# Block 0's gate and up of the second token pair by Strassen's seven products

## The chip, the cores and the metric

The kernel runs on one core of one Trainium2 chip. The metric is device time in microseconds (us), the median of several runs of one launch. Engines are called as in the profile: PE is TensorE's matmul stream and PEld its weight loads, DVE is VectorE, ACT is ScalarE, POOL is GpSimd, SP is SyncE, which here only issues DMAs.

## The reference

Two branches over the same x (2048 tokens, width 640) are mixed by a gate; the feed-forward width is 1728.

```python
a = jnp.einsum("bsd,ed->bse", x, dft_hid_re)
b = jnp.einsum("bsd,ed->bse", x, dft_hid_im)
y = jnp.einsum("ts,bse->bte", dft_seq_re, a) - jnp.einsum("ts,bse->bte", dft_seq_im, b)   # branch A
ffn = (gelu(x @ w_gate) * (x @ w_up)) @ w_down                                             # branch B
g = sigmoid((x * gate_w).sum(-1, keepdims=True))
out = g * y + (1 - g) * ffn
```

## The kernel before, in words

Every product is done in three matmuls: a float32 operand is split into a high part (a copy to the matmul's type, on ACT, `high`) and a low part (the rest, on DVE, `low`), and `mm3` adds high x high, high x low and low x high in a PSUM bank. There are eight banks of 128 x 512. Depth 640 is five tiles of 128; the 2048 tokens are two pairs of two tiles of 512 columns (pair 0 and pair 1, tile 1 and 2 of each); the width 1728 is 13 blocks of 128 and 64 rows more. Gate and up of these last 64 stand together in one "mixed" block of 128 rows: 64 of gate, 64 of up.

The order is: block 0 and the mixed block of the feed-forward; blocks 1 to 12; the down projection; branch A. Blocks 1 to 12 do gate and up by Strassen's algorithm in Winograd's form: tiles 0 to 3 of the depth are two halves (x pieces `(1,t)` and `(2,t)`), the four quarters of the problem are gate/up by token tile, and seven products of two depth tiles stand in for eight. The fifth depth tile (`x5`) is added plainly. For it the sums T1 to T4 of x pieces (`tsum`) and S1 to S4 and D of weights (`make_w`) are made on DVE, and each is split in its turn (`his`, `lows`).

Block 0 and the mixed block (`first_products`, `first_out`) are plain in the kernel before: for each token tile, five depth tiles by three blocks (m, g, u). Pair 0 is done as its data arrive; then tile 1 and tile 2 of pair 1. In this second stage the sums T1 to T4 of pair 0, T1 and T2 of pair 1 and all of block 1's weight parts are made beside the matmuls. `first_out` takes gelu of gate rows on ACT, multiplies by up rows on DVE, and stores the hidden rows to DRAM by a POOL DMA (`keep`). The mixed rows are multiplied twice, once into each half of a 128-row tile, so that the down projection finds them in both halves.

The first stages stand in one block `in_order(ACT, DVE, PE)`, which chains the instructions of each of these engines in the order of the program; blocks 1 to 12 stand in a second one, with POOL. The two chains of an engine are not tied to each other: the framework's scheduler merges them. In the second, work that is not matmul is spread between the products from a list with costs (`fills`; `todo` is put in it first). Big tiles (`slot`) come from a pool of 46 buffers of 4 KB per partition, given out in the order of the program as they come free.

The generator `gate_up` is the Strassen order for blocks 1 to 12, one per pair, whose steps the loop interleaves: X = A11 product of both pairs, a copy of X to V by ACT, V += A12 product and the fifth depth tile, Z = S1·T1, X += S2·T2, Z += D, X += S3·T3, then `s5 += X` on DVE, Z += S4, X += A22·T4, and the multiplies.

Of the kernel before, what the change touches and what calls it, by code (L numbers as in the profile page):

```python
# [9 lines left out]
F32 = mybir.dt.float32  # L10
F32R = mybir.dt.float32r
AF = mybir.ActivationFunctionType
ALU = mybir.AluOpType

P = 128
S, D, F = 2048, 640, 1728
T = 512
NT = S // T
ND = D // P
# [4 lines left out]
FR = F - NF * P  # L24
# [13 lines left out]
def kernel(  # L38
# [27 lines left out]
    nc = tc.nc  # L66
# [5 lines left out]
    def slot(dt, shape, name):  # L72
        return pool.tile(shape, dt, tag="s4", name=name, bufs=46)

    def mtile(dt, name):
        return pool.tile([P, T], dt, tag="m", name=name, bufs=14)

    def bank(name):
        return psum.tile([P, T], F32, tag="ps", name=name, bufs=8)

    def high(hi, raw):
        nc.scalar.activation(hi, raw, AF.Copy)  # L82

    def low(hi, lo, raw):
        nc.vector.tensor_tensor(lo, raw, hi.bitcast(F32), op=ALU.subtract)  # L85
# [13 lines left out]
    def mm3(ps, lhs, rhs, first, last):  # L99
        (lh, ll), (rh, rl) = lhs, rhs  # L100
        nc.tensor.matmul(ps, lh, rh, start=first, stop=False, skip_group_check=True)  # L101
        nc.tensor.matmul(ps, lh, rl, start=False, stop=False, skip_group_check=True)  # L102
        nc.tensor.matmul(ps, ll, rh, start=False, stop=last, skip_group_check=True)  # L103
# [19 lines left out]
    gwb = pool.tile([P, D], F32, tag="gwb", name="gwb")  # L123
# [18 lines left out]
    def at(hilo, i):  # L142
        h, l = hilo
        return h[:, i], l[:, i]

    def copy(src, name):
        m = mtile(F32, name)
        nc.scalar.activation(m, src, AF.Copy)  # L148
        return m
# [3 lines left out]
    def xpart(B, d, t):  # L153
        return at(B[1 + d // 2, t], d % 2) if d < 4 else at(B[5], t - 1)
# [47 lines left out]
    def wsmall(dt, name):  # L202
        return pool.tile([P, 2, P], dt, tag="w", name=name, bufs=6)
# [8 lines left out]
    def load_w(f):  # L212


        if f >= NF:
            return
        ra, rb = slot(F32, [P, 8, P], f"wa{f}r"), wsmall(F32, f"wb{f}")
        nc.sync.dma_start(ra, wf[f - 1, :, :8])
        nc.sync.dma_start(rb, wf[f - 1, :, 8:])
        rq = None  # L220
        if pair_of(f) == 1:
            rq = slot(F32, [P, 8, P], f"wq{f}r")
            nc.sync.dma_start(rq[:, 0:2], wf[f, :, 0:2])
            nc.sync.dma_start(rq[:, 2], wf[f, :, 4])
        wraw[f] = ra, rb, rq
# [147 lines left out]
        return W, work  # L373


    FIRST = [[(0, 1), (1, 3)], [(3, 6)], [(6, 8), (8, 9)], [(9, 12)], [(12, 15)]]

    def load_first():

        r, h, l = ([slot(dt, [P, 8, P], f"w0{n}{k}") for k in range(2)] for n, dt in (("r", F32), ("h", F32R), ("l", F32R)))  # L380
        W = {n: [tuple(v[c // 8][:, c % 8] for v in (h, l)) for c in range(k, 3 * ND, 3)] for k, n in enumerate("mgu")}

        def at8(v, a, b):
            return v[a // 8][:, a % 8 : a % 8 + b - a]

        def load(engine, a, b):
            engine.dma_start(at8(r, a, b), w0[:, a:b])

        def parts(do, a, b):
            if do is high:  # L390
                high(at8(h, a, b), at8(r, a, b))
            else:
                low(at8(h, a, b), at8(l, a, b), at8(r, a, b))

        return W, load, parts

    def keep(to, i, src):
        nc.gpsimd.dma_start(to[:, i], src)  # L398

    def first_banks(tp, t):  # L400
        return {n: bank(f"p{n}{tp}{t}") for n in "mgu"}

    def first_products(bk, W, B, t, ds=range(ND)):

        for d in ds:
            for n in "mgu":
                mm3(bk[n], W[n][d], xpart(B, d, t), d == 0, d == ND - 1)

    def first_out(bk, tp, t):
        ge, hf = mtile(F32, f"gem{tp}{t}"), mtile(F32, f"hfm{tp}{t}")  # L410
        nc.scalar.activation(ge[:FR], bk["m"][:FR], AF.Gelu_apprx_tanh)
        g = mtile(F32, f"ge{tp}{t}")
        nc.scalar.activation(g, bk["g"], AF.Gelu_apprx_tanh)
        tt(hf[:FR], ge[:FR], bk["m"][FR:], op=ALU.mult)
        tt(hf[FR:], ge[:FR], bk["m"][FR:], op=ALU.mult)
        keep(h0[tp], 1 + t, hf)
        tt(g, g, bk["u"], op=ALU.mult)
        keep(h0[tp], t - 1, g)

# [559 lines left out]
            put(2 * q + 1, 0, a[q])  # L979


    W0, load_part, parts = load_first()
    Bs = []
    B, tiles, load, piece, tsum, his, lows = load_x(0)

# [23 lines left out]
    def split_piece(d, t):  # L1009
        raw, _, hilo = piece(d, t)  # L1010
        split(*hilo, raw)

    with in_order(ACT, DVE, PE):
        nc.scalar.activation(table, table, AF.Gelu_apprx_tanh)
        idle = bank("idle")
        for k in range(14):
            nc.tensor.matmul(idle[:, halves[k % 2]], *ones, start=k == 0, stop=True, skip_group_check=True)
        bk1, bk2 = first_banks(0, 1), first_banks(0, 2)
        for d in range(ND):
            raw, _, (h, l) = piece(d, 1)  # L1020
            first, *rest = FIRST[d]
            parts(high, *first)
            if d == 0:
                a, b = halves
                nc.vector.tensor_copy(h[:, a], raw[:, a])
                low(h[:, a], l[:, a], raw[:, a])
                parts(low, *first)
                split(h[:, b], l[:, b], raw[:, b])
                parts(high, *rest[0])
                parts(low, *rest[0])  # L1030
            else:
                high(h, raw)
                parts(low, *first)
                low(h, l, raw)
                for r in rest:
                    parts(high, *r)
                for r in rest:
                    parts(low, *r)
            split_piece(d, 2)
            if d == 0:  # L1040
                wh, wl = W0["m"][0]
                for c in halves:
                    order = ((wh, h), (wl, h), (wh, l)) if c is halves[1] else ((wh, h), (wh, l), (wl, h))
                    for k, (w, x) in enumerate(order):
                        first = k == 0 and c is halves[0]
                        nc.tensor.matmul(bk1["m"][:, c], w, x[:, c], start=first, stop=False, skip_group_check=True)
                for n in "gu":
                    mm3(bk1[n], W0[n][0], (h, l), True, False)
            else:
                first_products(bk1, W0, B, 1, [d])  # L1050
            if d == 0:
                h, l = xpart(B, d, 2)
                for n in "mgu":
                    for k, w in enumerate(W0[n][d]):
                        nc.tensor.matmul(bk2[n], w, h, start=k == 0, stop=False, skip_group_check=True)
                for n in "mgu":
                    nc.tensor.matmul(bk2[n], W0[n][d][0], l, start=False, stop=False, skip_group_check=True)
            else:
                first_products(bk2, W0, B, 2, [d])
        B0, (tsum0, his0, lows0) = B, (tsum, his, lows)  # L1060
        Bs.append(B)
        B, tiles, load, piece, tsum, his, lows = load_x(1)
        tiles(1)
        load(1)
        tiles(2)
        load(2)
        tsum0(1)
        his((1, 1), (2, 1))
        lows((1, 1), (2, 1))
        split_piece(4, 1)  # L1070
        first_out(bk1, 0, 1)
        first_out(bk2, 0, 2)
        bk1 = first_banks(1, 1)
        first_products(bk1, W0, B, 1)
        tsum0(3)
        his0("T1", "T3")
        lows0("T1", "T3")
        tsum0(2)
        tsum0(4)
        his((1, 2), (2, 2))  # L1080
        lows((1, 2), (2, 2))
        split_piece(4, 2)
        his0("T2", "T4")
        lows0("T2", "T4")
        first_out(bk1, 1, 1)
        load_w(1)
        W, work = make_w(1)
        for _, do in work:
            do()
        load_w(2)  # L1090
        nc.sync.dma_start(gwb, gw.to_broadcast([P, D]))
        bk2 = first_banks(1, 2)
        first_products(bk2, W0, B, 2)
        tsum(1)
        his("T1")
        tsum(2)
        his("T2")
        lows("T1")
        first_out(bk2, 1, 2)

        todo.extend([(114, partial(lows, "T2")), (114, partial(tsum, 3)), (0, partial(his, "T3"))])
        todo.extend([(114, partial(tsum, 4)), (0, partial(his, "T4"))])
        todo.extend([(114, partial(lows, "T3")), (114, partial(lows, "T4"))])
    loads.close()
    Bs.append(B)
    zq = list(range(NS))
# [74 lines left out]
    with in_order(PE, ACT, DVE, POOL):  # L1181
        for f in range(1, NF):
# [80 lines left out]
            W = nxt  # L1263
# [438 lines left out]
```

## Time and profile before

| what | value |
|---|---|
| median of 3 runs | 1020.71 us (1020.39 to 1021.24) |
| span of the profiled execution, first to last instruction | 1019.2 us |
| PE busy | 1014.9 us, 4483 matmuls |
| DVE, ACT, POOL busy | 826.7, 485.1, 163.2 us |
| mean granted TensorE clock | 1.000 |
| products of pair 0, block 0 and mixed | until 25.65 us of the span |
| products of pair 1, block 0 and mixed | 25.65 to 46.05 us |
| block 1 | 46.05 to 70.55 us |

The profile gives one execution. Its own time is its span and 1.5 us around it, if it took as long as the median run. A row of the list in order of time reads: start, duration, engine, source line, operation, output tile <- input tiles, shapes, and in brackets the idle time of the engine before it with what ended it. A line such as L82 or L101 is a helper's (`high`, `mm3`), so rows are told apart by tile names: `x111h` is the high part of x of pair 1, piece 1, tile 1; `xT12l` the low part of pair 1's T2; `wa1`, `ws1` block 1's weights and their sums; `pm`, `pg`, `pu`, `pX`, `pV`, `pZ` PSUM banks. Matmuls are pipelined: a row's duration overlaps the next row, and the distance of two starts is what one costs.

### The profile page before, as it was taken

What the parts mean: (1) busy time and instruction counts of PE and PEld (TensorE: products, weight loads), DVE (VectorE), ACT (ScalarE), POOL (GpSimd) and SP (SyncE); (2) the same over time, 40 slices, a digit from 0 to 9 for tenths busy, and PEclk for the clock granted to TensorE, in tenths of its full rate; (3) what the DMA queues carried; (4) which work ended last, traced back from release to release, by engine and by line L of the source; (5) the groups of instructions that cost most, each with busy time, mean ns of one, the idle gap of its engine ahead of it and who ended that gap; (6) DMA issues with size and microseconds to landing.
All of it is one profiled execution on the core that took longest, in us unless ns stands there. A gap on an engine that the chain in (4) does not pass through costs nothing.

```text
span 1019.2 us, 13255 instructions
## 1 busy us (share of the span) xinstructions
PE 1014.9 (100%) x4483; PEld 840.1 (82%) x4483; DVE 826.7 (81%) x1158; ACT 485.1 (48%) x618; POOL 163.2 (16%) x291
## 2 busy tenths in 40 slices
PE   9999999999999999999999999999999999999998
PEld 7888888888888888888888888888888888888887
DVE  6987887977687979988887976898488859797796
ACT  5544535353535577557444443444344345455440
POOL 0122241323221200100001012102210200021121
PEclk9999999999999999999999999999999999999999
DMA  7468577968689999968874669658866877897855
GB/s 271 168 210 274 182 270 241 311 226 280 200 286 287 407 364 413 355 233 331 295 258 173 209 242 330 218 196 296 296 209 208 300 250 273 292 350 219 273 143 89
DMA packets 96068, 265.74 MB, mean 261 GB/s; under 512 B 12608, under 2 KB 26944, under 8 KB 96000
## 3 DMA queue, kind: packets, MB, share of 16 engines
q1 hardware_dynamic: 70512, 185.24, 52.9%
q0 software_dynamic: 25200, 79.46, 23.1%
q8 instruction: 35, 0.57, 0.2%
q14 instruction: 33, 0.27, 0.1%
q10 hardware_dynamic: 288, 0.20, 0.1%
HBM read 192.48 MB, written 70.27 MB: 258 GB/s over the span
## 4 chain that ended last, share of the span: by engine, by line
PE 100%; DVE 0%; issue 0%
PE pX L102 7%; PE pX L101 7%; PE pX L103 7%; PE pZ L101 5%; PE pZ L102 5%; PE pZ L103 5%; PE pL L103 3%; PE pL L101 3%; PE pL L102 3%; PE pV L103 2%; PE pV L101 2%; PE pV L102 2%; PE pR L103 1%; PE pY L103 1%; PE pQ L103 1%; PE pQ L101 1%
## 5 line engine op out<-in xcount | busy, mean ns | idle before, releaser
L82 ACT ACTIVATE ch<-csa 128x1024 fp32r<-128x1024 f32 x32 | 34.0, 1062 | 78.5 <-DVE csa L764 77.1
L85 DVE TENSOR_TENSOR cl<-cra,ch 128x1024 fp32r<-128x1024 f32 x32 | 39.1, 1222 | 27.0 <-ACT ch L82 24.9
L82 ACT ACTIVATE ch<-cra 128x1024 fp32r<-128x1024 f32 x32 | 33.9, 1059 | 52.3 <-DVE cl L85 16.3
L85 DVE TENSOR_TENSOR cl<-crb,ch 128x1024 fp32r<-128x1024 f32 x32 | 39.1, 1223 | 14.5 <-ACT ch L82 14.5
L103 PE MATMUL pL<-ch,xal 128*128 128x512 f32 x128 | 49.8, 389 | 0.0
L102 PE MATMUL pL<-cl,xah 128*128 128x512 f32 x128 | 49.8, 389 | 0.0
L101 PE MATMUL pL<-ch,xah 128*128 128x512 f32 x128 | 49.7, 389 | 0.0
L398 POOL DMA_DIRECT2D hA<-s x48 | 26.1, 544 | 138.1 <-DVE s L556 118.5
L82 ACT ACTIVATE ch<-crb 128x1024 fp32r<-128x1024 f32 x32 | 33.8, 1055 | 29.7 <-PE pL L102 11.6
L85 DVE TENSOR_TENSOR cl<-csb,ch 128x1024 fp32r<-128x1024 f32 x32 | 39.2, 1225 | 3.7 <-ACT ch L82 2.3
L85 DVE TENSOR_TENSOR cl<-csa,ch 128x1024 fp32r<-128x1024 f32 x32 | 39.1, 1221 | 2.1 <-ACT ch L82 1.1
L82 ACT ACTIVATE ch<-csb 128x1024 fp32r<-128x1024 f32 x32 | 34.0, 1062 | 11.7 <-DVE csb L767 5.0
L550 ACT ACTIVATE s<-s 128x512 f32<-128x512 f32 x24 | 15.2, 633 | 47.6 <-DVE s L549 47.6
L148 ACT ACTIVATE s<-pX 128x512 f32<-128x512 f32 x40 | 23.7, 596 | 29.0 <-PE pX L103 28.4
L82 ACT ACTIVATE kh<-kw 128x1024 fp32r<-128x1024 f32 x24 | 25.3, 1054 | 18.9 <-DMA kw<-wsd 14.5
L85 DVE TENSOR_TENSOR kl<-kw,kh 128x1024 fp32r<-128x1024 f32 x24 | 29.3, 1220 | 4.3 <-ACT kh L82 4.3
L545 DVE TENSOR_TENSOR s<-s,pX 128x512 f32<-128x512 f32 x24 | 16.4, 685 | 19.2 <-PE pX L103 19.1
L1349 POOL DMA_DIRECT2D uA<-c x8 | 4.3, 541 | 168.9 <-DVE c L1451 168.6
L398 POOL DMA_DIRECT2D hT<-s x48 | 26.0, 541 | 18.5 <-DVE s L573 8.1
L923 POOL DMA_DIRECT2D out<-ks x12 | 6.5, 541 | 137.4 <-DVE ks L922 136.5
L102 PEld LDWEIGHTS pL<-cl,xah 128*128 128x128 f32 x128 | 24.0, 188 | 5.0
L103 PEld LDWEIGHTS pL<-ch,xal 128*128 128x128 f32 x128 | 24.0, 188 | 5.0
(3626 smaller groups left out, 3479.0 us busy)
## 6 DMA issues: line engine op xcount, KB each, us to landing
cra<-in_ct SPq DMA_DIRECT2D x64, 512.0 KB, 4.2
crb<-in_ct SPq DMA_DIRECT2D x64, 512.0 KB, 5.0
hA<-s POOLq DMA_DIRECT2D x48, 256.0 KB, 5.7
hT<-s POOLq DMA_DIRECT2D x48, 256.0 KB, 5.0
kr<-hA SPq DMA_DIRECT2D x24, 512.0 KB, 7.7
kr<-hT SPq DMA_DIRECT2D x24, 512.0 KB, 7.3
ux<-uA SPq DMA_DIRECT2D x24, 512.0 KB, 6.2
ux<-uT SPq DMA_DIRECT2D x16, 512.0 KB, 7.3
```

What stands on the lines that cost most here:

```text
L82: nc.scalar.activation(hi, raw, AF.Copy)
L85: nc.vector.tensor_tensor(lo, raw, hi.bitcast(F32), op=ALU.subtract)
L101: nc.tensor.matmul(ps, lh, rh, start=first, stop=False, skip_group_check=True)
L102: nc.tensor.matmul(ps, lh, rl, start=False, stop=False, skip_group_check=True)
L103: nc.tensor.matmul(ps, ll, rh, start=False, stop=last, skip_group_check=True)
L148: nc.scalar.activation(m, src, AF.Copy)
L398: nc.gpsimd.dma_start(to[:, i], src)
L545: tt(s5, s5, X, op=ALU.add)
L550: nc.scalar.activation(s2, s2, AF.Gelu_apprx_tanh)
L923: nc.gpsimd.dma_start(acc4[:, t] if tp and e == 4 else out[2 * tp + t, e], src)
L1349: nc.gpsimd.dma_start(to[:, i], src)
```

## The change

Pair 1 of block 0 is done by the seven products. `load_first` now loads block 0's weights into three tiles of six chunks each instead of two of eight, and its new function `strassen` makes S1 to S4 and D from them; the mixed block's plain products stand between the seven. T2 to T4 of pair 0 are moved into block 1's `todo` list, T1 to T4 of pair 1 are made in this stage, and block 1's weight parts are made at its end. The loads of blocks 1 and 2's weights and of the gate's row are issued before the stage. The mixed rows are multiplied once and stored by two DMAs of 64 rows.

```diff
-    FIRST = [[(0, 1), (1, 3)], [(3, 6)], [(6, 8), (8, 9)], [(9, 12)], [(12, 15)]]
+    FIRST = [[(0, 1), (1, 3)], [(3, 6)], [(6, 9)], [(9, 12)], [(12, 15)]]
...
+        def strassen():
+            sm, sh, sl = (slot(dt, [P, 8, P], f"ws0{n}") for n, dt in (("r", F32), ("h", F32R), ("l", F32R)))
+            d, dr = wsmall(F32R, "wd0"), wsmall(F32, "wd0r")
+            (g01, u01), (g23, u23) = ([r[k][:, q:6:3] for q in (1, 2)] for k in range(2))
+            tt(sm[:, 0:2], u01, u23, op=ALU.add)
+            tt(sm[:, 4:6], g01, u01, op=ALU.subtract)
+            tt(sm[:, 2:4], sm[:, 0:2], g01, op=ALU.subtract)
+            tt(sm[:, 6:8], g23, sm[:, 2:4], op=ALU.subtract)
+            tt(dr[:, 0], r[2][:, 1], r[2][:, 2], op=ALU.subtract)
+            high(sh, sm)
+            high(d[:, 0], dr[:, 0])
+            low(sh, sl, sm)
+            low(d[:, 0], d[:, 1], dr[:, 0])
...
+    def mixed_out(ge, m, tp, t):
+        hf = mtile(F32, f"hfm{tp}{t}")
+        tt(hf[:FR], ge[:FR], m[FR:], op=ALU.mult)
+        for q in range(2):
+            nc.gpsimd.dma_start(h0[tp][q * FR : (q + 1) * FR, 1 + t], hf[:FR])
...
         split_piece(4, 1)
+        load_w(1)
+        load_w(2)
+        nc.sync.dma_start(gwb, gw.to_broadcast([P, D]))
+        S0 = first_strassen()
         first_out(bk1, 0, 1)
         first_out(bk2, 0, 2)
-        bk1 = first_banks(1, 1)
-        first_products(bk1, W0, B, 1)
-        tsum0(3)
-        his0("T1", "T3")
-        lows0("T1", "T3")
-        tsum0(2)
-        tsum0(4)
-        his((1, 2), (2, 2))
-        lows((1, 2), (2, 2))
-        split_piece(4, 2)
-        his0("T2", "T4")
-        lows0("T2", "T4")
-        first_out(bk1, 1, 1)
-        load_w(1)
-        W, work = make_w(1)
-        for _, do in work:
-            do()
-        load_w(2)
-        nc.sync.dma_start(gwb, gw.to_broadcast([P, D]))
-        bk2 = first_banks(1, 2)
-        first_products(bk2, W0, B, 2)
-        tsum(1)
-        his("T1")
-        tsum(2)
-        his("T2")
-        lows("T1")
-        first_out(bk2, 1, 2)
-        todo.extend([(114, partial(lows, "T2")), (114, partial(tsum, 3)), (0, partial(his, "T3"))])
-        todo.extend([(114, partial(tsum, 4)), (0, partial(his, "T4"))])
-        todo.extend([(114, partial(lows, "T3")), (114, partial(lows, "T4"))])
+        x1, x2 = at(B[5], 0), at(B[5], 1)
+        X, M1 = bank("pX0_1"), bank("pm11")
+        prod(X, "A11", (1, 1), True)
+        mixed(M1, 1, range(ND))
+        V = bank("pV0_1")
+        nc.scalar.activation(V, X, AF.Copy)
+        tsum(1)
+        his("T1")
+        lows("T1")
+        split_piece(4, 2)
+        prod(V, "A12", (2, 1), False)
+        mm3(V, S0["g5"], x1, False, True)
+        tsum(2)
+        his((1, 2), "T2")
+        lows((1, 2), "T2")
+        ge = mixed_gelu(M1, 1, 1)
+        his((2, 2))
+        s1 = mtile(F32, "s10_1")
+        nc.scalar.activation(s1, V, AF.Gelu_apprx_tanh)
+        lows((2, 2))
+        mixed_out(ge, M1, 1, 1)
+        Z, M2 = bank("pZ0_1"), bank("pm12")
+        prod(Z, "S1", "T1", True)
+        mm3(Z, S0["u5"], x2, False, True)
+        s5 = copy(Z, "s50_1")
+        mixed(M2, 2, range(2))
+        prod(X, "S2", "T2", False)
+        tsum(3)
+        his("T3")
+        lows("T3")
+        s2 = copy(X, "s20_1")
+        mm3(Z, S0["D"], x2, False, False)
+        mixed(M2, 2, range(2, ND))
+        prod(X, "S3", "T3", False)
+        tsum(4)
+        his("T4")
+        lows("T4")
+        W, work = make_w(1)
+        sums, high_a, sums2, high_c, low_a, diff, low_c = (do for _, do in work)
+        high_a()
+        ge = mixed_gelu(M2, 1, 2)
+        mixed_out(ge, M2, 1, 2)
+        tt(s5, s5, X, op=ALU.add)
+        prod(Z, "S4", (2, 2), False)
+        prod(X, "A22", "T4", False)
+        mm3(X, S0["u5"], x1, False, True)
+        low_a()
+        tt(s2, s2, Z, op=ALU.add)
+        nc.scalar.activation(s2, s2, AF.Gelu_apprx_tanh)
+        sums()
+        tt(s2, s2, s5, op=ALU.mult)
+        keep(h0[1], 1, s2)
+        sums2()
+        high_c()
+        his0("T1")
+        tt(s1, s1, X, op=ALU.mult)
+        keep(h0[1], 0, s1)
+        lows0("T1")
+        low_c()
+        diff()
+        for k in (2, 3, 4):
+            todo.extend([(114, partial(tsum0, k)), (0, partial(his0, f"T{k}")), (114, partial(lows0, f"T{k}"))])
```

More of the change, by code (lines that the diff above doesn't have):

```diff
@@ L373, in make_w @@
         return W, work
-    FIRST = [[(0, 1), (1, 3)], [(3, 6)], [(6, 8), (8, 9)], [(9, 12)], [(12, 15)]]
+    FIRST = [[(0, 1), (1, 3)], [(3, 6)], [(6, 9)], [(9, 12)], [(12, 15)]]
     def load_first():
-        r, h, l = ([slot(dt, [P, 8, P], f"w0{n}{k}") for k in range(2)] for n, dt in (("r", F32), ("h", F32R), ("l", F32R)))
-        W = {n: [tuple(v[c // 8][:, c % 8] for v in (h, l)) for c in range(k, 3 * ND, 3)] for k, n in enumerate("mgu")}
+        r, h, l = ([slot(dt, [P, 8, P], f"w0{n}{k}") for k in range(3)] for n, dt in (("r", F32), ("h", F32R), ("l", F32R)))
+        W = {n: [tuple(v[c // 6][:, c % 6] for v in (h, l)) for c in range(k, 3 * ND, 3)] for k, n in enumerate("mgu")}
         def at8(v, a, b):
-            return v[a // 8][:, a % 8 : a % 8 + b - a]
+            return v[a // 6][:, a % 6 : a % 6 + b - a]
         def load(engine, a, b):
@@ L393, in parts @@
                 low(at8(h, a, b), at8(l, a, b), at8(r, a, b))
-        return W, load, parts
+        def strassen():
[11 more added lines that the diff above has]
+            low(d[:, 0], d[:, 1], dr[:, 0])
+            S = {"D": (d[:, 0], d[:, 1]), "g5": W["g"][4], "u5": W["u"][4]}
+            for i in range(2):
+                S["A11", i], S["A12", i], S["A22", i] = W["g"][i], W["g"][2 + i], W["u"][2 + i]
+                for k in range(4):
+                    S[f"S{k + 1}", i] = at((sh, sl), 2 * k + i)
+            return S
+        return W, load, parts, strassen
     def keep(to, i, src):
@@ L407, in first_products, with mixed_gelu @@
                 mm3(bk[n], W[n][d], xpart(B, d, t), d == 0, d == ND - 1)
+    def mixed_gelu(m, tp, t):
+        ge = mtile(F32, f"gem{tp}{t}")
+        nc.scalar.activation(ge[:FR], m[:FR], AF.Gelu_apprx_tanh)
+        return ge
+    def mixed_out(ge, m, tp, t):
[3 more added lines that the diff above has]
+            nc.gpsimd.dma_start(h0[tp][q * FR : (q + 1) * FR, 1 + t], hf[:FR])
     def first_out(bk, tp, t):
-        ge, hf = mtile(F32, f"gem{tp}{t}"), mtile(F32, f"hfm{tp}{t}")
-        nc.scalar.activation(ge[:FR], bk["m"][:FR], AF.Gelu_apprx_tanh)
+        ge = mixed_gelu(bk["m"], tp, t)
         g = mtile(F32, f"ge{tp}{t}")
         nc.scalar.activation(g, bk["g"], AF.Gelu_apprx_tanh)
-        tt(hf[:FR], ge[:FR], bk["m"][FR:], op=ALU.mult)
-        tt(hf[FR:], ge[:FR], bk["m"][FR:], op=ALU.mult)
-        keep(h0[tp], 1 + t, hf)
+        mixed_out(ge, bk["m"], tp, t)
         tt(g, g, bk["u"], op=ALU.mult)
@@ L979, in step_k @@
             put(2 * q + 1, 0, a[q])
-    W0, load_part, parts = load_first()
+    W0, load_part, parts, first_strassen = load_first()
     Bs = []
@@ L1084, with prod, mixed @@
-        lows0("T2", "T4")
-        first_out(bk1, 1, 1)
-        load_w(1)
-        W, work = make_w(1)
-        for _, do in work:
-            do()
-        load_w(2)
-        nc.sync.dma_start(gwb, gw.to_broadcast([P, D]))
-        bk2 = first_banks(1, 2)
-        first_products(bk2, W0, B, 2)
+        def prod(ps, a, b, first):
+            for i in range(2):
+                mm3(ps, S0[a, i], at(B[b], i), first and i == 0, True)
+        def mixed(ps, t, ds):
+            for d in ds:
+                mm3(ps, W0["m"][d], xpart(B, d, t), d == 0, True)
```

## The prediction

> **What bounds the kernel now.** I read the page first (busy shares, the chain that ended last), then busy time by window over the start, where the change lies, then the instructions there in order of time, engine by engine.
>
> ```profile
> PE 1014.9 (100%) x4483; PEld 840.1 (82%) x4483; DVE 826.7 (81%) x1158; ACT 485.1 (48%) x618; POOL 163.2 (16%) x291
> PE 100%; DVE 0%; issue 0%
> 25.65:46.05 20.40, 20.40 (x91) 16.89 (x90) 19.85 (x25) 10.19 (x13) 3.09 (x6) 1.00 0.57 209
> 46.05:70.55 24.50, 24.50 (x109) 20.26 (x108) 19.91 (x27) 12.60 (x19) 2.71 (x5) 1.00 0.48 154
> ```
>
> The last two rows give window, length, busy time and count of PE, PEld, DVE, ACT, POOL, granted clock, DMA share, GB/s. TensorE alone sets the time. The first window is the second token pair's plain stage, 90 matmuls (x91 counts a straddler) in 20.40 us: 0.2267 us each. The second is block 1, 108 matmuls. PE never waits, so a matmul saved counts in full, and so does a wait. But VectorE is busy 19.85 of 20.40 us in the stage that is rewritten.
>
> ```profile
> 25.65 0.39 PE L101 MATMUL pm<-x111h,w0h 128*128 128x512 f32 x1
> 25.88 0.39 PE L102 MATMUL pm<-x111l,w0h 128*128 128x512 f32 x1
> 46.05 0.39 PE L101 MATMUL pX<-x011h,wa1h 128*128 128x512 f32 x1
> ```
>
> **The change, part by part.** (1) Matmuls. Before: 5 depth tiles x 3 blocks x 3 x 2 token tiles = 90. After: mixed block 30, seven products 42, leftover depth tile 4 x 3 = 12: 84. Six fewer: -6 x 0.2267 = -1.36 us. The Trainium skill ("TensorE: Matmul & The Clock Gate", "Wait — 56ns, not 53.3ns?") gives 215.7 ns for such a matmul; an estimate from that page would be -1.29; the rows decide.
>
> (2) VectorE and ScalarE up to the new products:
>
> ```profile
> 19.38 0.69 DVE L85 TENSOR_TENSOR x15l<-xr,x15h 128x512 fp32r<-128x512 f32 x1
> 23.08 0.69 DVE L414 TENSOR_TENSOR hfm<-gem,pm 64x512 f32<-64x512 f32 x1 [3.01 <-ACT gem L411]
> 23.78 0.69 DVE L415 TENSOR_TENSOR hfm<-gem,pm 64x512 f32<-64x512 f32 x1
> 26.65 0.69 DVE L417 TENSOR_TENSOR ge<-ge,pu 128x512 f32<-128x512 f32 x1
> 27.25 1.22 DVE L184 TENSOR_TENSOR xs<-xr,xr 128x1024 f32<-128x1024 f32 x1
> 28.39 1.22 DVE L85 TENSOR_TENSOR xT01l<-xs,xT01h 128x1024 fp32r<-128x1024 f32 x1
> 40.41 0.42 DVE L277 TENSOR_TENSOR ws1r<-wb,wa1r 128x256 f32<-128x256 f32 x1
> 41.88 1.22 DVE L85 TENSOR_TENSOR wa1l<-wa1r,wa1h 128x1024 fp32r<-128x1024 f32 x1
> 41.99 1.06 ACT L82 ACTIVATE ws1h<-ws1r 128x1024 fp32r<-128x1024 f32 x1 [5.07 <-DVE ws1r L283]
> 43.01 0.28 DVE L296 TENSOR_TENSOR wb<-wa1r 128x128 f32<-128x128 f32 x1
> ```
>
> A 1024-column DVE pass takes 1.22, and the next starts 1.14 later (27.25, 28.39); a 512 pass 0.6 to 0.7; four weight sums 1.47 (40.41 to 41.88); a high pass on ACT 1.06. The new weight sums start when x15l leaves DVE, 19.99, in what was an idle of 3.01: sums to 21.7, high to 22.63, low to 23.89, the small difference to 24.0. Then first_out's two tiles, with one 64-row multiply each where there were two (23.08, 23.78): its last multiply starts at 26.12 (before 26.65). Cost: nothing, the idle covers it; without that cover these 3.2 us of DVE work would move (3) by as much. The first weights' merged pass in FIRST saves some 0.15 on DVE, where the x15 pair is what it waits for: nothing. DVE reaches T1 at 26.73.
>
> (3) From there the code runs sum (DVE), high (ACT), low (DVE) with little between:
>
> ```profile
> 45.02 1.22 DVE L184 TENSOR_TENSOR xs<-xr,xr 128x1024 f32<-128x1024 f32 x1
> 46.33 1.06 ACT L82 ACTIVATE xT11h<-xs 128x1024 fp32r<-128x1024 f32 x1 [2.69 <-DVE xs L184]
> 47.43 1.23 DVE L85 TENSOR_TENSOR xT11l<-xs,xT11h 128x1024 fp32r<-128x1024 f32 x1
> ```
>
> Sum to low is 2.4 us here (45.02 to 47.43), so DVE idles 1.2 at each of T1, T3, T4. By these prices DVE starts: T1 26.73, its low 29.1, x15 low 30.2, T2 30.8, lows of x12, T2 and x22 at 32.0, 33.2 and 34.65, mixed multiply 35.8, T3 36.5, its low 38.85 (ends 40.07), T4 40.0, its low 42.35 (ends 43.57), second mixed multiply 43.78 (its gelu stands behind wa1's high on ACT), s5 += X 44.48 (ends 45.17). PE, gapless, does 63 matmuls from 25.65 and reaches S3 at 39.94; S3's second matmul, 40.17, needs T3's low: just in time. S3 and S4 end at 42.67. A22 adds into the bank that s5 += X must have read: PE waits to 45.21, 2.54 us. Block 1's first two matmuls need only wa1's high part (43.26) and may run in the gap; the third needs wa1's low, queued on DVE behind s5. So +2.54 - 0.45 = **+2.09**. Ends: 1.6 (0.5 faster over the dozen steps) and 3.4 (no matmul pulled forward, and another 0.85 of a block 1 sum slipped in on DVE). I take the rows' sum.
>
> (4) The end. Behind s5 DVE still holds wa1's low, s2 += Z, four weight sums, two multiplies, the lows of T1 (first pair) and ws1, and the difference; ACT two highs and the difference's high. Block 1's V products need ACT's copies of X. Block 1 is ordered separately from block 0, and the two may interleave on an engine, as before:
>
> ```profile
> 47.61 0.58 ACT L515 ACTIVATE pV<-pX 128x512 f32<-128x512 f32 x1 [0.22 <-PE pX L103]
> 48.11 1.05 ACT L82 ACTIVATE xT12h<-xs 128x1024 fp32r<-128x1024 f32 x1
> 49.06 0.58 ACT L411 ACTIVATE gem<-pm 64x512 f32<-64x512 f32 x1
> 49.53 0.58 ACT L413 ACTIVATE ge<-pg 128x512 f32<-128x512 f32 x1
> 50.01 0.59 ACT L515 ACTIVATE pV<-pX 128x512 f32<-128x512 f32 x1
> ```
>
> The first V copy, block 1's, went ahead of xT12h and gem, block 0's: whatever is ready first goes. So: A22 ends 47.25, X of pair 0 48.16, of pair 1 49.52; the copy runs at 48.4 while ACT waits for the weight sums (49.2); then T2's high of pair 0 (48.9), ws1's (49.8), T1's (50.8), the second copy 51.7 to 52.30. PE, through V of pair 0 at 51.56, waits **0.78**; then Z waits **0.26** for ws1's low (54.6). Ends: 0 (both copies ahead of the highs, weights in time) and 2.25 + 0 (first copy behind ws1's and T1's highs: 51.14 to 51.73 against 49.52). I take 1.04, by readiness.
>
> (5) Sums moved into block 1: three sums and three lows of pair 0 (6 x 1.14) for two sums and three lows of pair 1: +1.14 on DVE and one more high. Block 1's 4.6 us of DVE idle (24.50 - 19.91) covers it: T2's low about 51 against its product at 58.7, T3's 56 against 62.8, T4's 60 against 68.3. Without cover PE would wait up to 1.14.
>
> (6) Queues.
>
> ```profile
> 24.80 0.70 POOL L398 DMA_DIRECT2D h<-hfm  x1 [24.36 <-DVE hfm L415]
> 15.29 0.34 SPq L218 DMA_DIRECT2D wa1r<-in_wf  x1
> 32.02 0.33 SPq L218 DMA_DIRECT2D wa2r<-in_wf  x1
> ```
>
> Four stores of mixed rows become eight: four more issues of up to 0.70 on POOL, busy 3.09 of 20.40, read first in block 2: nothing, or that much if POOL were late. T4's store of pair 0 moves from 33 to about 57, read in block 3: nothing. On SP the loads of wa1, wa2 and the gate row move ahead, queued behind x; x12 is wanted at 26.7, so they cost nothing unless they delay it by 5 us. Block 0's weights hold nine buffers of the 46 where they held six, and their sums three more; block 3's weights may load later, with a block to spare.
>
> **Sum**: -1.36 + 2.09 + 1.04 = +1.8 us. Against the profile's span of 1019.2 that is 1021.0; the median of the runs, 1020.71, lies 1.5 above the span: **1022.5**, 0.18% slower, just inside the 0.2% (2.04 us) that a measurement can tell.
>
> **Rivals.** (a) Block 0's tail fits: s5 += X ends by 44.4 and the copies are never late; idle stays under the 1.36 saved, and with none the time is 1019.35. It decides at 0.8 us less DVE chain than I add up. For it: 1.2 us holes in that chain; against: each hole is a hand-over that the code orders. (b) The first V copy stands behind both highs: -1.36 + 2.09 + 2.25 = +3.0, 1023.7. For it: wa1's sums and X of block 1 come ready within 1 us of each other. (c) ACT keeps block 0's whole order, the difference's high (53.9) included: V starts at 54.7 instead of 49.52, 5.2 us: 1026.6. Against: the rows at 47.61. (d) The idle PE drops to a slow clock:
>
> ```profile
> 5.16 0.63 PE L101 MATMUL pg<-x011h,w0h 128*128 128x512 f32 x1
> 5.59 0.63 PE L102 MATMUL pg<-x011l,w0h 128*128 128x512 f32 x1
> 7.02 0.39 PE L103 MATMUL pu<-x011h,w0l 128*128 128x512 f32 x1
> ```
>
> At the start matmuls come 0.43 apart (5.16, 5.59), until about 6.8. Six us at that pace lose 6 x (1 - 0.2267/0.43) = 2.8: 1025.3. The Trainium skill (same page, "Why this matters for your kernels") warns of gaps above about 3 us; mine are two of 0.6 and 1.5. No row here shows a gap in mid-run.
>
> **How the numbers follow.** Forecast 0.55 (0.36 within 0.2%, 0.19 slower by its terms' spread), (a) 0.13 (0.03 faster by a shorter stage than I count, 0.10 same), (b) 0.20 (0.18 slower), (c) 0.06, (d) 0.06. Same 0.48, slower 0.49, faster 0.03. The range 1019.3 to 1025.0 takes in (a) and (b); (c) and (d) are left out. The forecast's own range is 1021.2 to 1023.5.
>
> **What would show it.** Right: PE idle before pX's A22 group released by DVE's s5 += X, about 1.5 to 2.5 us; T3's low within 0.3 us of S3; a second, smaller idle before the V or Z of block 1, released by ACT or DVE; 4477 matmuls. Wrong: no PE idle between 25 and 60 us (a), one of 2 us or more before V (b, c), matmuls 0.43 apart behind a gap (d), or idle in block 1's later groups (5).

## The result and the profile after

The changed kernel takes 1028.45 us (median of 5 runs, 1027.47 to 1030.59) against 1020.77 us before: ratio 1.0076, 95% interval 1.0065 to 1.0087. It is 7.7 us slower, outside the range; the forecast was 1.8 us slower. The five runs go with the mean clock that TensorE was granted, as a share of full speed: 0.998 at 1027.47 and 1027.48, 0.997 at 1028.45 and 1028.46, 0.995 at 1030.59.

The page of the changed kernel (busy shares, the chain that ended last), then its list of what TensorE waited for: total us, times, longest.

```profile
PE 1016.5 (99%) x4477; PEld 839.7 (82%) x4477; DVE 828.7 (81%) x1162; ACT 488.4 (48%) x622; POOL 166.3 (16%) x295
PE 96%; DVE 2%; ACT 1%; DMA 0%; issue 0%; SPq 0%; ACTq 0%
PE pV L101 <- ACT pV L545: 4.6, 1, 4.6
PE pX L101 <- DVE s L1158: 1.2, 1, 1.2
PE pX L101 <- ACT wa1h L82: 0.3, 1, 0.3
```

The six matmuls are gone (4477). But the chain is no longer PE alone. The three waits are the places that the prediction named: A22 behind s5 (line 1158), block 1's first matmuls behind wa1's high part, and V behind its copy, only that the last is 4.6 us; the wait of 0.26 before Z that it added is not there. TensorE's rows around them:

```profile
42.00 0.39 PE L103 MATMUL pZ<-x122h,ws0l 128*128 128x512 f32 x1
42.65 0.50 PE L101 MATMUL pX<-x011h,wa1h 128*128 128x512 f32 x1 [0.26 <-ACT wa1h L82]
42.99 0.40 PE L102 MATMUL pX<-x011l,wa1h 128*128 128x512 f32 x1
44.57 0.50 PE L101 MATMUL pX<-xT14h,w0h 128*128 128x512 f32 x1 [1.19 <-DVE s L1158]
44.90 0.39 PE L102 MATMUL pX<-xT14l,w0h 128*128 128x512 f32 x1
...
50.83 0.39 PE L103 MATMUL pV<-x05h,wa1l 128*128 128x512 f32 x1
55.83 0.80 PE L101 MATMUL pV<-x121h,wa1h 128*128 128x512 f32 x1 [4.62 <-ACT pV L545]
56.43 0.63 PE L102 MATMUL pV<-x121l,wa1h 128*128 128x512 f32 x1
...
61.81 0.40 PE L103 MATMUL pZ<-xT01h,ws1l 128*128 128x512 f32 x1
```

By distances of starts, each less the 0.2269 that a matmul takes (44.93 us for 198 before): 42.00 to 44.90 holds 4 matmuls and 1.99 us more; 50.83 to 55.83 holds 4.77 more; and from 55.83 to 61.81 the matmuls are 0.43 apart, 14 distances and 2.80 more. Against 1020.77: -1.36 + 1.99 + 4.77 + 2.80 = +8.2. The profiled execution also reached pair 1's products 0.46 earlier than the one before (25.19 for 25.65), which leaves the measured +7.7. Why the copy was late stands in the rows of ScalarE and VectorE:

```profile
47.85 0.58 ACT L545 ACTIVATE pV<-pX 128x512 f32<-128x512 f32 x1 [0.94 <-PE pX L103]
48.47 1.06 ACT L82 ACTIVATE ws1h<-ws1r 128x1024 fp32r<-128x1024 f32 x1
49.43 1.04 ACT L82 ACTIVATE xT01h<-xs 128x1024 fp32r<-128x1024 f32 x1
53.10 0.31 ACT L82 ACTIVATE wd<-wb 128x128 fp32r<-128x128 f32 x1 [2.63 <-DVE wb L296]
54.24 1.06 ACT L82 ACTIVATE xT02h<-xs 128x1024 fp32r<-128x1024 f32 x1 [0.83 <-DVE xs L184]
55.20 0.58 ACT L545 ACTIVATE pV<-pX 128x512 f32<-128x512 f32 x1
51.65 1.22 DVE L85 TENSOR_TENSOR ws1l<-ws1r,ws1h 128x1024 fp32r<-128x1024 f32 x1
52.99 1.22 DVE L184 TENSOR_TENSOR xs<-xr,xs 128x1024 f32<-128x1024 f32 x1
```

The second pV row is pair 1's copy. It stands behind T2's high pass (xT02h), and that waits for T2's sum, which VectorE makes at 52.99, behind the whole tail of block 0. ScalarE idles 2.63 and 0.83 us while the copy's input has been ready since about 49.2. The first of the two idles ends with the high pass of block 0's weight difference (wd); the run a_late tells which of the two passes held the copy. The granted clock by windows (columns: window, length, busy time of PE, PEld, DVE, ACT and POOL with counts, granted clock, DMA share, GB/s):

```profile
54.00:55.00 1.00, 0.00 (x0) 0.00 (x0) 0.41 (x2) 0.76 (x1) 0.00 (x0) 0.89 0.00 0
55.00:56.00 1.00, 0.17 (x1) 0.17 (x1) 0.67 (x1) 1.00 (x3) 0.00 (x0) 0.50 0.00 0
...
61.00:62.00 1.00, 1.00 (x4) 0.76 (x4) 0.22 (x1) 0.00 (x0) 0.37 (x1) 0.70 0.00 0
```

A mean of 0.89 between 54 and 55 is a fall from 1.00 to 0.50 at 54.78, if it came in one step, some 3.6 us after the last matmul was done (50.83 + 0.39 = 51.22). At 61 to 62 a mean of 0.70 puts the rise at 61.6, after 5.8 us of unbroken work.

### The profile page after: what moved, and what is told of

The parts are those of the page before. It is cut to its first block, busy times and chain, and to the rows that moved or that the text cites. A ratio compares the mean times of both kernels' runs of the same rounds, so it can differ in the third digit from the quotient of the medians.

```text
span 1026.7 us, 13246 instructions
## 1 busy us (share of the span) xinstructions
PE 1016.5 (99%) x4477; PEld 839.7 (82%) x4477; DVE 828.7 (81%) x1162; ACT 488.4 (48%) x622; POOL 166.3 (16%) x295
## 4 chain that ended last, share of the span: by engine, by line
PE 96%; DVE 2%; ACT 1%; DMA 0%; issue 0%; SPq 0%; ACTq 0%
PE pX L103 7%; PE pX L101 7%; PE pX L102 7%; PE pZ L101 5%; PE pZ L103 5%; PE pZ L102 5%; PE pL L103 3%; PE pL L102 3%; PE pL L101 3%; PE pV L101 2%; PE pV L103 2%; PE pV L102 2%; PE pR L102 1%; PE pQ L102 1%; PE pY L102 1%; PE pY L103 1%
## 5 line engine op out<-in xcount | busy, mean ns | idle before, releaser
L148 ACT ACTIVATE s<-pX 128x512 f32<-128x512 f32 x41 | 24.3, 596 | 29.0 <-PE pX L103 28.5
L561 ACT ACTIVATE s<-pZ 128x512 f32<-128x512 f32 x24 | 14.2, 595 | 31.0 <-PE pZ L103 25.9
```

Source lines behind the costliest of these rows:

```text
L561: nc.scalar.activation(s5, Z, AF.Copy)
```

## The experiments

All ratios are to the kernel before, run beside each on the same chip; medians in us.

| run | median | before beside it | ratio (95%) |
|---|---|---|---|
| a_late | 1023.21 | 1020.83 | 1.0023 (1.0013 to 1.0033) |
| c_both | 1023.75 | 1020.83 | 1.0024 (1.0015 to 1.0033) |
| d_warm | 1025.82 | 1020.83 | 1.0049 (1.0036 to 1.0061) |
| e_hole | 1024.66 | 1020.83 | 1.0040 (1.0027 to 1.0052) |
| h_group | 1020.28 | 1020.62 | 0.9996 (0.9986 to 1.0005) |
| k_t1 | 1019.57 | 1020.62 | 0.9990 (0.9981 to 0.9999) |
| f_rest | 1020.16 | 1020.62 | 0.9994 (0.9986 to 1.0003) |
| n_s5late | 1020.97 | 1020.66 | 1.0002 (0.9993 to 1.0011) |
| p_gap | 1027.68 | 1020.66 | 1.0066 (1.0053 to 1.0078) |

**a_late: the T2 sum issued behind both copies**

```diff
+        todo.append((228, lambda: None))
         for k in (2, 3, 4):
             todo.extend([(114, partial(tsum0, k)), (0, partial(his0, f"T{k}")), (114, partial(lows0, f"T{k}"))])
```

> The changed kernel with one entry more at the head of block 1's list of work: it does nothing and costs 228, so that the sum and the split of pair 0's T2 are issued behind block 1's two copies of X, not between them. Theory (the second copy stood on ScalarE behind T2's high pass, which waited for a sum at the end of VectorE's queue; the 4.6 us of TensorE idle then lowered the clock): the copy runs at about 50.5, the idle before V of pair 1 and the slow clock both go, 4.6 to 5.0 plus 2.5: about 1021.0 us. Rival 1 (the slow clock has another cause than this idle): only the idle goes, about 1023.7. Rival 2 (VectorE and ScalarE are simply too late for block 1, and the wait moves to Z or to the T2 product): less than half is gained, 1025 or more.

The wait for the copy and the slow clock are both gone (granted clock 0.999 or 1.0 in all nine runs), and 5.2 of the expected 7.4 us. The time is nearest to rival 1's 1023.7, but that rival had the slow clock stay. Of the 2.2 us that are left, 1.3 are a wait that was not there: block 1's S3 now waits for ScalarE's copy of X. From the list of waits, and ScalarE's rows:

```profile
PE pX L101 <- ACT s L148: 1.3, 1, 1.3
PE pX L101 <- DVE s L1158: 1.2, 1, 1.2
50.64 0.58 ACT L545 ACTIVATE pV<-pX 128x512 f32<-128x512 f32 x1
53.36 0.31 ACT L82 ACTIVATE wd<-wb 128x128 fp32r<-128x128 f32 x1 [1.26 <-DVE wb L296]
61.52 1.06 ACT L82 ACTIVATE xT04h<-xs 128x1024 fp32r<-128x1024 f32 x1 [1.45 <-DVE xs L184]
62.48 1.06 ACT L148 ACTIVATE s<-pX 128x512 f32<-128x512 f32 x2
```

Pair 1's copy runs at 50.64, ahead of the difference's high pass, which comes as late as in the changed kernel (53.36, there 53.10). So it was T2's high pass that held the copy, and not the difference's. The wait before S3 is the same pattern one step on: the two copies (L148) stand behind T4's high pass, which waits 1.45 for T4's sum.

**c_both: a_late, and s5 += X into the hole before T4's low pass**

```diff
         his("T4")
+        tt(s5, s5, X, op=ALU.add)
         lows("T4")
 ...
         mixed_out(ge, M2, 1, 2)
-        tt(s5, s5, X, op=ALU.add)
```

> As the run before, and s5 += X is moved on VectorE from behind T4's low pass and the mixed multiply to the hole between T4's sum and its low pass. Theory (TensorE's first wait is for s5, 1.2 us in the list of waits): s5 is done at about 41.8, A22 then waits only for T4's low pass, some 0.5 us, so about 1 us less than the run before: 1020.0. Rival (the wait is for T4's low pass as much as for s5): no gain, 1021.0.

The wait before A22 is gone, the median is not lower, and both forecasts, which stood on a_late's, missed:

```profile
PE pX L101 <- ACT s L148: 1.8, 1, 1.8
PE pZ L103 <- DVE ws1l L85: 0.5, 1, 0.5
```

TensorE comes to Z and S3 earlier and waits longer there, 0.5 for ws1's low pass and 1.8 for the copy: 2.3 where a_late waited 1.3, so 1.0 of the 1.2 gained at A22 goes back. The eleven runs fall into two groups by their mean granted clock: four at 1.0 took 1022.32 to 1022.82, seven at 0.998 took 1023.44 to 1024.30. So most of the spread goes with the slow clock: a mean of 0.998 over 1022 us is, as an estimate, 4 us at 0.50, and the groups' medians are 1.3 us apart. At the full clock c_both is 0.75 us under a_late, of which the waits give 0.2. Which idle lowers the clock no trace shows: the profiled run (1022.35) is one of the four, and of its waits in block 1 none is longer than 1.8.

**d_warm: TensorE kept at work in the wait**

```diff
+                    if f == 1 and (step, tp) == (1, 0):
+                        warm = bank("warm")
+                        for k in range(40):
+                            nc.tensor.matmul(warm[:, halves[k % 2]], *ones, start=k == 0, stop=True, skip_group_check=True)
                     if (step, tp) in ((0, 1), (1, 1)):
```

> The changed kernel, with 40 matmuls of 256 columns on constants put behind V of pair 0 in block 1, into a bank that nothing reads: they keep TensorE running in some 4.4 us of the 4.6 us wait and change no order on VectorE and ScalarE. Theory (half clock from about 54.8 to 61.4 is the price of the idle): the wait stays and the clock does not fall, 2.5 to 2.8 less than the changed kernel: 1025.8. Rival (the slow matmuls have another cause, or the idle is all of the loss): 1028.4, no change.

As expected, to the tenth, with a granted clock of 1.0 in all five runs. V of pair 1 starts as late as in the changed kernel, and there its matmuls follow each other at the full clock's pace, with rows of 0.40 where the changed kernel's had 0.63:

```profile
50.96 4.66 PE L1320 MATMUL warm<-const-bfloat16-1.0 128*128 128x256 bf16 x40
55.75 0.50 PE L101 MATMUL pV<-x121h,wa1h 128*128 128x512 f32 x1
56.09 0.40 PE L102 MATMUL pV<-x121l,wa1h 128*128 128x512 f32 x1
```

So 2.6 us of the loss (1028.45 to 1025.82) is the clock, and it falls because TensorE idles.

**e_hole: T2's sum made in VectorE's hole at T3**

```diff
         his("T3")
+        tsum0(2)
         lows("T3")
 ...
-        for k in (2, 3, 4):
+        todo.extend([(0, partial(his0, "T2")), (114, partial(lows0, "T2"))])
+        for k in (3, 4):
             todo.extend([(114, partial(tsum0, k)), (0, partial(his0, f"T{k}")), (114, partial(lows0, f"T{k}"))])
```

> The changed kernel with pair 0's T2 sum made in VectorE's hole between T3's sum and T3's low pass; its high and low passes head block 1's list. The scheduler now puts T2's high pass ahead of the first copy of X. Theory: the first copy runs at about 51.4 (behind three high passes), TensorE waits about 3.0 us before V of pair 0 in place of 4.6 before V of pair 1, and none or little later. If the clock holds over 3.0 us of idle: 1024.0. If it falls there too: 1026.6. Rival (the sum's place has no part in it): 1028.4.

The wait moves to the first copy and is 2.85 us. In the profiled run (1024.33) and two more the granted clock is 1.0; the two slowest, 1025.42 and 1025.64, read 0.998, so in them it fell, at a place that no trace shows:

```profile
52.38 0.50 PE L101 MATMUL pV<-x021h,wa1h 128*128 128x512 f32 x1 [2.85 <-ACT pV L545]
```

So the sum's place has its part, against the rival. But an earlier sum alone does not free the copies: T2's high pass now stands ahead of the first one (50.81, the copy 51.75).

**h_group: sums grouped in block 1's list**

```diff
         todo.append((228, lambda: None))
-        for k in (2, 3, 4):
-            todo.extend([(114, partial(tsum0, k)), (0, partial(his0, f"T{k}")), (114, partial(lows0, f"T{k}"))])
+        todo.extend([(114, partial(tsum0, 2)), (114, partial(tsum0, 3)), (0, partial(his0, "T2", "T3")), (114, partial(lows0, "T2"))])
+        todo.extend([(114, partial(tsum0, 4)), (0, partial(his0, "T4")), (114, partial(lows0, "T3")), (114, partial(lows0, "T4"))])
```

> The run with the late T2 and the early s5, and pair 0's T2 to T4 issued in block 1 as two sums ahead of two high passes (T2 sum, T3 sum, T2 and T3 high, T2 low, T4 sum, T4 high, T3 low, T4 low) in place of sum, high, low for each. Theory (the wait before block 1's S3, 1.8 us there, is ScalarE's copy of X standing behind T4's high pass, which waits for T4's sum; the three hand-overs of 1.2 us on VectorE make that late): T4's high pass ends some 3 us sooner, the 1.8 us go, the 0.5 us before Z stays: about 1.8 less than that run, 1020.5 to 1022.0. Rival (VectorE has too much work in block 1 and the wait moves to A22): no gain.

On top of c_both; 1020.28. No wait for the copy of X is left, only the one for ws1's low pass (0.5), and T4's high pass starts at 57.99 where it started at 60.85 in c_both:

```profile
57.99 1.06 ACT L82 ACTIVATE xT04h<-xs 128x1024 fp32r<-128x1024 f32 x1 [0.73 <-DVE xs L184]
```

The gain is 3.5 us between the medians, but c_both's median is one of its runs at the slow clock. Against its four at the full clock it is 2.2, against its profiled run 1.9, near the 1.8 of the wait; all runs of h_group read 1.0.

**k_t1: T1 of pair 0 split where the engines idle**

```diff
         s5 = copy(Z, "s50_1")
+        his0("T1")
 ...
         his("T3")
+        lows0("T1")
         lows("T3")
 ...
         high_c()
-        his0("T1")
         tt(s1, s1, X, op=ALU.mult)
         keep(h0[1], 0, s1)
-        lows0("T1")
         low_c()
```

> As the grouped run, and the high and low pass of pair 0's T1 are taken from the end of the stage and put where the engines idle: the high pass on ScalarE behind the copy of Z, the low pass on VectorE between T3's sum and T3's low pass. Theory: no wait of TensorE over 0.3 us is left but a part before A22, and the six matmuls saved show: 1020.8 - 1.36 = 1019.5, up to 1020.2 with restarts. Rival (T3's low pass comes later and S3 waits, or the kernel is slower for a reason outside these waits): 1021 or more.

On top of h_group; 1019.57, the lower end. It is the fastest of all: 1.05 us under the kernel before beside it, 0.6 under f_rest (below). Its starts around A22 are 0.37 too far apart (42.07 to 43.12, three distances), so the rows give -1.36 + 0.37 = -1.0. Its page, then rows of TensorE and VectorE:

```profile
PE 1013.6 (100%) x4477; PEld 837.6 (82%) x4477; DVE 828.8 (81%) x1162; ACT 488.1 (48%) x622; POOL 165.8 (16%) x295
PE 100%; DVE 0%; issue 0%
42.07 0.39 PE L101 MATMUL pX<-xT14h,w0h 128*128 128x512 f32 x1
43.12 0.39 PE L103 MATMUL pX<-xT14h,w0l 128*128 128x512 f32 x1
36.77 1.21 DVE L85 TENSOR_TENSOR xT01l<-xs,xT01h 128x1024 fp32r<-128x1024 f32 x1
37.98 1.22 DVE L85 TENSOR_TENSOR xT13l<-xs,xT13h 128x1024 fp32r<-128x1024 f32 x1
```

The chain is PE alone again, and VectorE does T1's low pass in the hole before T3's without moving it (37.98; 38.13 in the changed kernel).

**f_rest: all of the change but the seven products**

```diff
+    FIRST = [[(0, 1), (1, 3)], [(3, 6)], [(6, 9)], [(9, 12)], [(12, 15)]]   # three tiles of six chunks
 ...
-        tt(hf[FR:], ge[:FR], bk["m"][FR:], op=ALU.mult)
-        keep(h0[tp], 1 + t, hf)
+        for q in range(2):
+            nc.gpsimd.dma_start(h0[tp][q * FR : (q + 1) * FR, 1 + t], hf[:FR])
 ...
+        load_w(1)
+        load_w(2)
+        nc.sync.dma_start(gwb, gw.to_broadcast([P, D]))
         first_out(bk1, 0, 1)
```

> The kernel before with every part of the change but the seven products: the merged pass and three tiles for block 0's weights, the loads of blocks 1 and 2's weights and of the gate's row ahead, the mixed rows multiplied once and stored twice. Theory (prediction's steps 2 and 6: these cost nothing): 1020.8, within 0.4. Rival (four more POOL issues, the earlier loads or the buffers cost): 1021.5 or more; or four multiplies less on a full VectorE gain: nothing, since TensorE never waited.

1020.16, 0.5 lower, and the interval of the ratio holds 1: these parts cost nothing.

**n_s5late: the wait for s5 alone.** k_t1 with the two s5 lines of c_both's diff put back.

> The kernel without waits (grouped sums, T1 early), with s5 += X put back behind T4's low pass and the mixed multiply on VectorE, as in the change. It prices the prediction's step 3 by itself. Theory: TensorE waits before A22 as in the changed kernel, where the starts around it are 2.0 us more apart than the matmuls take: 1019.57 + 2.0 = 1021.6, one wait for s5 of about 1.2 in the list and 0.3 before block 1's first matmuls. Rival (the wait is T4's low pass, not s5): 1019.6 to 1020.

1020.97, 1.4 us over k_t1 where 2.0 were expected. The stretch that held 1.99 us too much in the changed kernel holds 1.94 here (42.52 to 45.37, four distances), but k_t1 has 0.37 of that too, so 1.57 are the wait's. The waits are the two that were expected; below them the two rows of TensorE:

```profile
PE pX L101 <- DVE s L1160: 1.2, 1, 1.2
PE pX L101 <- ACT wa1h L82: 0.2, 1, 0.2
42.52 0.39 PE L103 MATMUL pZ<-x122h,ws0l 128*128 128x512 f32 x1
45.37 0.40 PE L102 MATMUL pX<-xT14l,w0h 128*128 128x512 f32 x1
```

**p_gap: an idle of 3.3 us.** d_warm with `range(12)`.

> The changed kernel with 12 of the 256-column matmuls on constants behind V of pair 0 where the earlier run had 40: TensorE works 1.4 us longer and then idles some 3.4 us, between the 2.85 us at which the clock held and the 4.6 us at which it fell (it fell 3.6 us into the idle in the changed kernel's profile). Theory (the clock falls by the length of the idle, and 3.4 is about its limit): some runs at 1025.8 and some at 1027 to 1028.5; a median of 1025.8 says that 3.4 us is short enough. Rival (it falls at any idle of 3 us or more): 1028.0 in all runs.

```profile
51.66 1.51 PE L1320 MATMUL warm<-const-bfloat16-1.0 128*128 128x256 bf16 x12
56.43 0.50 PE L101 MATMUL pV<-x121h,wa1h 128*128 128x512 f32 x1 [3.26 <-ACT pV L545]
```

In the profiled run, 1026.37, the clock held over 3.26 us of idle. The other four took 1027.10 to 1027.80 and read 0.998, so in them it fell. That is the mixture that the theory expected, 0.6 us later at its fast end, and not the rival's fall in all runs. How long the four idled, and where the clock fell, no trace shows.

## Why the prediction was wrong, point by point

- Step 1, -1.36: right, as far as the runs can tell. With no wait left in the list (k_t1) the change is 1.05 us under the kernel before, the interval of the ratio being 0.1 to 1.9 us; the rows give 1.0 less.
- Step 2, nothing: right. VectorE reached T1 at 26.06, forecast 26.73, in an execution whose second stage began 0.46 earlier (25.19 for 25.65).
- Step 3, +2.09: right in place, order and size. Less that 0.46, T3's low pass, T4's and s5 start within 0.3 us of the forecast; the starts are 1.99 apart too much, with the two matmuls of block 1 in the gap. Put back alone it costs 1.4 (n_s5late), since 0.37 of it stays without the wait.
- Step 4, +1.04: this is the step that failed. The first copy ran ahead of ws1's and T1's high passes as said. The second was put at 51.7, "by readiness", with T2's high pass ahead of it at 48.9. But T2's high needs T2's sum, and the step never placed that sum on VectorE; it comes at 52.99, behind block 0's tail. The rule from the rows of before (whatever is ready first goes) held between the two ordered blocks. Inside block 1 the order is fixed: sum, high pass and copy follow each other there, so the copy cannot pass a high pass that is not ready. That is 4.77 us in place of 1.04. Shown by a_late, where only T2's sum and passes are issued later, behind the copies, and the wait goes.
- Step 5, covered: wrong, and hidden in the changed kernel. The sums have time enough by VectorE's load, but each high pass blocks ScalarE's copies behind it. Once TensorE comes on time, S3 waits 1.3 to 1.8 (a_late, c_both), and grouping the sums removes it (h_group).
- Step 6, nothing: right (f_rest).
- Rival (c), 1026.6, had nearly the size of the idle (5.2), but at the wrong copy and behind the wrong instruction: the difference's high pass does run ahead of the copy in the changed kernel, but a_late shows that it does not hold it. Rival (d), the slow clock, was given 0.06 and came with it: 2.8 forecast from the start's rows, 2.80 in the changed kernel's rows, 2.6 in d_warm. That the two 2.8 agree is partly luck: how long the slow clock lasts was carried over from the start, where no idle comes before it. The two were counted as alternatives; the long idle brings the slow clock, so their prices add, and a range that ended at 1025 left both out. The warning of the Trainium skill that rival (d) cites, on gaps above about 3 us ("TensorE: Matmul & The Clock Gate", "Why this matters for your kernels"), agrees with the profiled executions: the clock held at 2.85 and 3.26 us of idle and fell at 4.62. It is no sharp line here: the clock also fell in two of five runs of e_hole, four of five of p_gap and seven of eleven of c_both, and for c_both no trace shows an idle near 3 us.

What stays open: why the scheduler left T2's sum out of the holes that VectorE had at T4's hand-over and at 49, and which idle lowers the clock in seven of c_both's runs.

## What to carry to other kernels

When work is moved into a later stage's list, follow every instruction of it to the engine that issues it, and ask which short instruction stands behind it there: a copy that a matmul needs costs nothing by its own length and microseconds behind a pass that is not ready. On an engine that works in order, group independent sums ahead of their passes, and put passes into hand-over holes, so that nothing waits in front of such a copy. Price a TensorE idle of about 3 us or more with the slow clock behind it, and read the clock of every run: a median can be of runs at the slow clock while the profiled run is not.

## What the runs showed of the hardware that was not expected

The slow clock outlasts the idle: after 4.62 us without matmuls it stood at 0.50 from 54.78 to 61.6, 5.8 us of them with TensorE at work without a break, at 0.43 us a matmul. Matmuls on constants into an unused bank, 40 of 256 columns in 4.66 us, held it at 1.0.

One kernel can meet the slow clock in some runs and not in others: c_both, e_hole and p_gap each have runs at a mean of 1.0 and runs at 0.998, and the latter take 1.0 to 1.3 us longer.
